# The first stage's operations, recorded and issued in the order of a planner inside the kernel

## The chip, the cores and the metric

One core of one Trainium2 chip runs the whole program. The metric is the device time of one execution in microseconds (us); lower is better. Three executions of the kernel before took 850.84, 848.12 and 849.52 us: the median is 849.52 us. One more execution was taken with the hardware profiler, and all rows below come from it.

The engines have the profile's names: PE is the matrix engine (PEld its weight loads), DVE the vector engine, ACT the activation engine, POOL the general one, SP the queue that issues most of the DMAs. Each takes its instructions strictly in the order of its own list; an instruction that waits holds up all that stand behind it.

## The reference, cut to what matters

Four layers stand one after the other on x of 2048 positions and 512 channels, each added to x:

```python
x = A_q
x = x + _A_ref(_layernorm(x), A_k, A_v, A_shift_k, A_ssm_k, A_ssm_D)
x = x + _B_ref(_layernorm(x), B_log_A_real, B_A_imag, ...)
x = x + _A_ref(_layernorm(x), A_k, A_v, A_shift_k, A_ssm_k, A_ssm_D)
x = x + _B_ref(_layernorm(x), B_log_A_real, B_A_imag, ...)
# _A_ref: kv = (4-tap causal convolution of k) * v
#         y  = long causal convolution of kv with ssm_k (FFT of 4096) + kv * ssm_D;  q * y
# _B_ref: K[d, l] = 2 Re sum_n C[d, n] exp(A[d, n] dt[d] l), l = 0 .. 2047, n = 0 .. 127
#         y  = long causal convolution of u with K + u * D_skip
```

The convolution inside A and the kernel K of B are the same in both rounds, since neither depends on x.

## The kernel before, in words

All lines are those of the kernel before. Long convolutions are done as Fourier transforms by matrix products. Channels come in four quarters of 128 (NQ), a quarter's frequencies in eight chunks (NCH). There are three parts:

- **The prologue** (lines 354 to 444) turns the parameters of B into four rows per mode, splits each into a high and a low half (`split`, line 378) and writes them to DRAM (`rows_d`, line 383).
- **The first stage** (lines 447 to 745) runs two streams of work, which `run_steps` (line 924) records in turns, two steps of one and three of the other.
- **The rest** (from line 748) is the first round's B, then the second round's A and B, and takes what the first stage wrote to DRAM (`spec`, `ya_d`, `x1_d`).

The first stage's streams:

- `stream()` (line 599) makes K. 64 **taps** in 16 groups of four: `load_rows` (line 470) loads a group's rows (`raw`) and casts them to `rw` on DVE (line 478); `mags` (line 480) makes magnitudes, a matmul and an Exp on ACT (line 488), six for every eight taps; `angles` (line 493) makes a tap's angles in a bank `pa` of PSUM by two matmuls (lines 497 and 502) with a rounding on DVE between them (line 501); `waves` (line 505) takes one Abs and five sines on ACT (lines 509 to 514); `products` (line 518) multiplies twice on POOL (lines 525 and 526) and once on DVE (line 527, which frees the bank `pa`, of which there are two); `contract` (line 531) sums over the modes on PE (line 539), and after a group's fourth tap writes the group to DRAM (`kdram`, line 551). After each 16 taps `spectrum_quarter(1, q)` (line 249) loads the quarter back (`kk`, line 221), adds D_skip on POOL (line 265), transforms it (lines 179, 188, 197), copies it out on ACT (line 278) and writes it as `spec` (line 279).
- `diagonal()` (line 708) does A: first `spectrum_quarter(0, q)` of ssm_k, beside 16 groups of the short convolution, `gated` (line 620: eight multiplications and additions in SBUF, four on POOL and four on DVE, all eight on POOL for the first group), and the statistics of x (`row_stats`, line 643); then `convolution(0, ...)` (line 284): spectra of kv (lines 179 and 188), the products with `kab` (loaded at line 294; lines 306, 308, 309), the way back (lines 211, 318, 332, 338) and the gate (lines 692, 693, 704). `ln_rows` (line 674) runs four times within it: it loads four rows of x for each partition (`xr`, one buffer), normalizes them by four instructions on ACT (line 679) and writes them to `ln_d` (line 681).

Exps and sines need different tables on ACT; `after` (line 113) keeps each set together by an edge in the order, without a wait.

**What sets the order.** Each call of an operation is traced at once, in the order in which the two streams are recorded. A scheduler of the framework (`schedule_with_timeline_sim=True`, line 982) then sets the place of each instruction on its engine by a priority and a model of times of its own, over the whole program, and puts in the semaphores. PSUM and SBUF tiles with the same tag share a few buffers: `f1` (two buffers, line 451) holds in turn the results of lines 179, 197, 211 and 486.

Of the kernel before, what the change touches and what calls it, by code (L numbers as in the profile page):

```python
# [100 lines left out]


@with_exitstack
def kernel(ctx: ExitStack, tc: tile.TileContext, out, x_in, kv_in, ssmk_in, ssmd_in,
                           la_in, ai_in, cr_in, ci_in, ldt_in, ldtb_in, dsk_in,
                           w1_in, w2_in, mm_in, w4_in, minus_in, tt_in, tg1_in, tg2_in, dbg=None):
    nc = tc.nc
    V, S, G, T = nc.vector, nc.scalar, nc.gpsimd, nc.tensor

    def sbuf(stack, name, side="left"):  # L110
        return stack.enter_context(tc.tile_pool(name=name, bufs=1, side=side, reuse_waits="tile"))

    def after(ins, first):
        tc.add_manual_dep(ins.ins, first.ins.name,
                          mybir.DependencyInfo(mybir.DependencyClass.NoSync, mybir.DependencyReason.DATA),
                          reason="activation tables")

# [11 lines left out]
    GL = 2  # L129
# [87 lines left out]
    def by_half(tile_, rows, store=False):  # L217
        src = rows.rearrange("(a b n) y -> b n a y", a=2, b=2)
        for b in range(2):
            ends = tile_[64 * b:64 * b + 64], src[b]  # L220
            nc.sync.dma_start(*(ends[::-1] if store else ends))

# [26 lines left out]
    def spectrum_quarter(which, q, src, pool, zlast, zb):  # L249
        z = pool.tile([128, 64, 32, 2], F32, name="zk", tag="z", bufs=zb)  # L250
        dr = pool.tile([1, 128], F32, name="dr", tag="dr", bufs=1)
        nc.sync.dma_start(dr, (ssmd_in, dsk_in)[which][:, 128 * q:128 * q + 128])
        for g in range(4):
            kk = pool.tile([128, 512], F32, name="kk", tag="kk", bufs=(NKK, 2)[which])
            by_half(kk, src[4 * q + g])
            d = dr[:, 32 * g:32 * g + 32]
            if which == 0:
                kv = kk.rearrange("p (t c) -> p t c", c=32)
                view = lambda ps_, j, n: kv[ps_, :, j:j + n]
            else:  # L260
                kv = kk.rearrange("p (i t c) -> p t i c", i=4, c=8)
                view = lambda ps_, j, n: kv[ps_, :, j // 8:(j + n) // 8, :]
                d = d.rearrange("p (i c) -> p i c", c=8)

            G.tensor_add(kv[0:1, 0], kv[0:1, 0], d)
            fwd_group(view, z, 32 * g, zlast[-zb] if len(zlast) >= zb else None)
            yield
        for c in range(NCH):
            if c % 2 == 0:
                pu, ins = f2_pair(z, c)  # L270
                if c == NCH - 2:
                    zlast.append(ins)

            if which == 1 and q == NQ - 1:
                pc = wk.tile([128, CK * 128], F32, name="pc", tag="m1", bufs=NM1 // 2)
            else:
                pc = pool.tile([128, CK * 128], F32, name="pc", tag="pc", bufs=2)
            S.copy(pc, pu[:, c % 2].rearrange("p k c -> p (k c)"))  # L278
            nc.sync.dma_start(spec[which][q][c], pc)
            yield  # L280
# [3 lines left out]
    def convolution(which, pools, steps, finish, lag, ahead, nk, ns, nw, inplace, zlast=None, late_step=None, first_b=False):  # L284
# [3 lines left out]
        def load(s):  # L288
            q, c = divmod(s, NCH)
            pool = pools["conv"]  # L290
            kab = pool.tile([128, 2, CK, 128], F32, name="kab", tag="kab", bufs=nk)
            eng = G if first_b and s < GL else nc.sync
            rows = spec[which][q][c].rearrange("(f v) x -> f (v x)", v=2)
# [69 lines left out]
    dt = gp.tile([128, 4], F32, name="dt")  # L363
    nc.sync.dma_start(dt, ldt_in)
    nc.sync.dma_start(flat(cr), cr_in)
    nc.sync.dma_start(flat(ci), ci_in)
    nc.sync.dma_start(flat(la), la_in)
    nc.sync.dma_start(flat(ai), ai_in)
    nc.sync.dma_start(w1, w1_in)
    dt2 = gp.tile([128, NQ, 32], F32, name="dt2")  # L370
# [7 lines left out]
    def split(i, v, eng):  # L378
# [3 lines left out]
        eng.tensor_sub(hl[:, 1], v, hl[:, 0])  # L382
        nc.sync.dma_start(rows_d[k].rearrange("q (h r x) g n -> r (q h) x (g n)", h=2, r=2)[r]
                          .rearrange("a (c p) y -> a c (p y)", p=2),
# [56 lines left out]
    nc.sync.dma_start(flat(dt2), ldtb_in[:, None, :].to_broadcast([4, 32, 128]))  # L441
    S.activation(dt2, dt2, AF.Exp)
# [8 lines left out]
    psum["f1"] = (pp, 2)  # L451

    wk = sbuf(gctx, "wk")
    kp = sbuf(gctx, "spec_k")
# [15 lines left out]
    def load_rows(gi):  # L470
        if gi in rows:
            return
        raw = wk.tile([128, 2, 128], F32, name="raw", tag="raw", bufs=2)
        q, g = divmod(gi, 4)
        for k in range(2):
            nc.sync.dma_start(raw[:, k, :], rows_d[k][q, :, g, :])
        rows[gi] = wk.tile([128, 2, 128], F32R, name="rw", tag="rw", bufs=2)
        V.tensor_copy(rows[gi], raw)
# [52 lines left out]
    def contract(gi, k):  # L531
# [18 lines left out]
        for i4 in range(4):  # L550
            nc.sync.dma_start(
                kdram[gi].rearrange("(s n) (i x) -> i n s x", n=32, i=4)[i4],
# [57 lines left out]
    with ExitStack() as actx:  # L610
# [9 lines left out]
        def gated(grp, onpool):  # L620
# [16 lines left out]
            e[7].tensor_mul(u, u, kt(19))  # L637
            nc.sync.dma_start(kv_d[grp], u.rearrange("p t c -> p (t c)"))
            yield
# [12 lines left out]
        def steps_a(q):  # L652
# [3 lines left out]
            def load(g):  # L656
                us[g] = ap.tile([128, 16, 32], F32, name="u", tag="kk", bufs=NKK)
                nc.sync.dma_start(us[g].rearrange("p t c -> p (t c)"), kv_d[4 * q + g])

# [14 lines left out]
        def ln_rows(j):  # L674
# [5 lines left out]
            for q in range(NQ):  # L680
                nc.sync.dma_start(ln_d[q][:, 4 * j:4 * j + 4, :], xr[:, :, 128 * q:128 * q + 128])

        xqs = {}

        def load_x(q):
            xqs[q] = ap.tile([128, 16, 128], F32, name="xq", tag="xq", bufs=1)
            nc.sync.dma_start(xqs[q], ln_d[q])

# [6 lines left out]
        def stats_a(q, c):  # L695
# [3 lines left out]
            if c == 6:  # L699
                nc.sync.dma_start(x1_d[q], xqs[q])  # L700

        def finish_a(q, g, po):
            ya = ap.tile([128, 512], F32, name="ya", tag="pc", bufs=2)
            S.copy(ya, po.rearrange("p t c -> p (t c)"))
            nc.sync.dma_start(ya_d[:, :, 4 * q + g].rearrange("k p x -> p k x"), ya.rearrange("p (k x) -> p k x", k=4))
            update_a(q, g, po)

        def diagonal():
            kvs = kv_steps()
            for q in range(NQ):  # L710
                for i, _ in enumerate(spectrum_quarter(0, q, ssmk_in, ap, zlast, ZA)):
# [4 lines left out]
                    if q == 0 and i < 4:  # L716
                        nc.sync.dma_start(w2[:, 8 * i:8 * i + 8], w2_in[:, 8 * i:8 * i + 8])
                    if q == 2 and i < 4:
                        ins = nc.sync.dma_start(mm[:, 8 * i:8 * i + 8], mm_in[:, 8 * i:8 * i + 8])
                        after(ins, zlast[0])  # L720
                    if q == 3 and i == 0:
                        after(nc.sync.dma_start(w4, w4_in), zlast[0])
                    next(kvs, 0)
# [19 lines left out]
        for _ in range(4):  # L743
            next(diag)
        run_steps([(stream(), RT), (diag, RD)])


# [3 lines left out]
    def gated_update(buffer, spare, rnd):  # L751
        yas = []
        for k in range(4):
            ya = buffer(k)
            nc.sync.dma_start(ya.rearrange("p g t c -> p (g t c)"), ya_d[k].rearrange("p g x -> p (g x)"))
            yas.append(ya)
# [47 lines left out]
    for q in range(NQ):  # L804
        nc.sync.dma_start(x[:, :, 128 * q:128 * q + 128], x1_d[q])
    last_root[0] = normalizer(0, 16, st_all)
# [180 lines left out]
```

## Time and profile before

| | |
|---|---|
| median of three runs | 849.52 us (848.12 to 850.84) |
| profiled execution, whole | 858.07 us |
| its span, from first to last instruction | 856.2 us |
| mean granted PE clock | 0.821 |
| DVE, ACT, POOL busy | 541.8, 433.9, 401.0 us |
| moved by DMA | 147.35 MB, mean 172 GB/s |

The first stage's last operations run at about 600 us. A row of a timeline or of the chain of waits begins with its start and its length in us. A group's row gives line, engine, operation, result<-operands and count, then busy time, mean length (ns), and the idle time just ahead of the group with what ended it. A row of stretches gives for each engine the busy time and, in brackets, the count, and then the granted clock of PE, the share of DMA and GB/s. A source row gives shortest, median and longest length in ns.

### The profile page before, as it was taken

Reading aid. Unit: us, or ns where it says so; the run is one execution under the profiler, and the core shown is the slowest. Engines: PE = TensorE matmul, PEld = TensorE weight load, DVE = VectorE, ACT = ScalarE, POOL = GpSimd, SP = SyncE. Lnnn points to the kernel's source line nnn. Section 1 sums busy time; section 2 is a strip of 40 time slices with the busy share of each in tenths; the row PEclk is TensorE's granted clock in tenths of the full one; section 3 lists DMA queues with packets and bytes.
Section 4 is the critical chain, followed back from the end, with each engine's and each line's share of the span. In section 5 each row is a group of like instructions: output and inputs, shape, how many; then the busy total and the mean of one; then the engine's idle time right before and its main releaser. Section 6 shows DMA issues by size and latency. Waiting matters only on the chain.

```text
span 856.2 us, 20760 instructions
## 1 busy us (share of the span) xinstructions
PE 564.1 (66%) x8440; PEld 325.6 (38%) x8440; DVE 541.8 (63%) x931; ACT 433.9 (51%) x800; POOL 401.0 (47%) x362
## 2 busy tenths in 40 slices
PE   2336664556747765358978667886379895469985
PEld 0014233323424422136534434552136562136562
DVE  7858888783544443134777562477457798987874
ACT  3126344435636783385774527552566341856431
POOL 4859989943332622227734422542035351045451
PEclk9999999657776556757997977797689998689998
DMA  9865844543345335765656553554978573127874
GB/s 249 200 179 156 280 138 155 172 146 121 108 142 179 104 85 137 177 192 158 215 148 226 185 163 121 162 173 122 279 241 283 200 248 99 49 57 257 259 233 88
DMA packets 77635, 147.35 MB, mean 172 GB/s; under 512 B 8668, under 2 KB 37732, under 8 KB 74980
## 3 DMA queue, kind: packets, MB, share of 16 engines
q1 hardware_dynamic: 76676, 143.60, 54.9%
q0 software_dynamic: 864, 2.43, 0.8%
q8 instruction: 67, 1.10, 0.5%
q14 instruction: 28, 0.23, 0.1%
HBM read 101.95 MB, written 44.04 MB: 171 GB/s over the span
## 4 chain that ended last, share of the span: by engine, by line
PE 23%; DVE 14%; ACT 14%; issue 10%; DMA 9%; POOL 2%; SPq 1%; POOLq 0%; ACTq 0%; DVEq 0%
PE pi L211 7%; PE pu L197 4%; DMA kab<-spec 4%; PE po L338 3%; PE pf L179 3%; PE pk L539 2%; DVE w L332 2%; PE pa L502 2%; DVE vv L309 2%; ACT m L488 2%; DVE zu L188 2%; DMA kk<-kdram 2%; ACT ab L509 1%; DMA ln_d<-xr 1%; DVE x L774 1%
## 5 line engine op out<-in xcount | busy, mean ns | idle before, releaser
L308 POOL TENSOR_TENSOR sw<-sw,kab 128x512 f32<-128x512 f32 x96 | 121.0, 1281 | 141.7 <-ACT sw L306 131.8
L525 POOL TENSOR_TENSOR xy<-tt,m 128x512 f32<-128x512 f32 x64 | 76.2, 1191 | 139.6 <-issue 69.7
L527 DVE TENSOR_TENSOR e<-pa,m 128x512 f32<-128x512 f32 x64 | 43.8, 684 | 109.4 <-ACT pa L514 109.3
L211 PE MATMUL pi<-vv,mm 64*64 64x128 f32 x1536 | 89.1, 288 | 9.5 <-DVE vv L309 3.0
L211 PE MATMUL pi<-sw,mm 64*64 64x128 f32 x1536 | 88.5, 285 | 5.3 <-POOL sw L308 3.1
L309 DVE TENSOR_TENSOR vv<-pu,kab 128x512 f32<-128x512 f32 x96 | 62.1, 680 | 44.7 <-ACT sw L306 28.9
L539 PE MATMUL pk<-xy,e 128*32 128x64 f32 x2048 | 61.4, 271 | 39.7 <-POOL xy L526 26.8
L509 ACT ACTIVATE ab<-pa 128x512 f32<-128x512 f32 x64 | 38.2, 597 | 97.3 <-PE pa L502 96.8
L179 PE MATMUL pf<-kk,w 64*128 64x512 f32 x128 | 62.6, 960 | 30.9 <-DMA kk<-ssmk_in 20.4
L497 PE MATMUL pa<-tt,rw 64*128 64x512 f32 x64 | 42.0, 659 | 61.2 <-DVE e L527 61.1
L526 POOL TENSOR_TENSOR xy<-tt,m 128x512 f32<-128x512 f32 x64 | 79.1, 1237 | 0.0
L179 PE MATMUL pf<-u,w 64*128 64x512 f32 (+1 forms) x200 | 64.3, 713 | 19.7 <-ACT pc L278 9.7
L188 DVE STREAM_TRANSPOSE zu<-pf 128x512 f32<-128x512 f32 x96 | 62.3, 689 | 22.9 <-PE pf L179 22.7
L539 PEld LDWEIGHTS pk<-xy,e 128*32 128x32 f32 x2048 | 45.3, 139 | 78.8 <-POOL xy L526 41.5
L488 ACT ACTIVATE m<-pm 128x1024 f32<-128x1024 f32 x48 | 47.1, 1027 | 50.7 <-PE pm L486 50.5
L338 PE MATMUL po<-w,w 128*64 128x512 f32 x192 | 60.0, 714 | 18.1 <-DVE xq L693 10.8
L197 PE MATMUL pu<-zu,w 64*64 64x128 f32 x1536 | 61.4, 293 | 15.3 <-DVE zu L188 13.7
L211 PEld LDWEIGHTS pi<-vv,mm 64*64 64x64 f32 x1536 | 57.3, 140 | 34.6 <-issue 20.8
L306 ACT COPY sw<-pu 128x1024 f32<-128x1024 f32 x48 | 48.7, 1015 | 37.7 <-PE pu L197 37.5
L197 PEld LDWEIGHTS pu<-zu,w 64*64 64x64 f32 x1536 | 50.3, 145 | 38.5 <-issue 21.0
L211 PEld LDWEIGHTS pi<-sw,mm 64*64 64x64 f32 x1536 | 61.2, 142 | 8.4 <-issue 4.6
L318 ACT COPY ie<-pi 128x1024 f32<-128x1024 f32 x32 | 32.4, 1013 | 60.6 <-PE pi L211 60.6
(141 smaller groups left out, 1125.9 us busy)
## 6 DMA issues: line engine op xcount, KB each, us to landing
kab<-spec SPq DMA_DIRECT2D x94, 512.0 KB
spec<-pc SPq DMA_DIRECT2D x64, 256.0 KB
kvt<-kv_in SPq DMA_DIRECT2D x32, 312.0 KB
kk<-ssmk_in SPq DMA_DIRECT2D x32, 128.0 KB
xr<-x_in SPq DMA_DIRECT2D x8, 512.0 KB
kv_d<-u SPq DMA_DIRECT2D x16, 256.0 KB
kdram<-ks SPq DMA_DIRECT2D x64, 64.0 KB
kk<-kdram SPq DMA_DIRECT2D x32, 128.0 KB
```

Of the source, the lines that this page charges most:

```text
L179: yield T.matmul(o, w1[half, :], rhs, start=True, stop=True)
L188: V.transpose(zr[:, :, r], pf[..., r].rearrange("p a x t -> p x a t"))
L197: ins = T.matmul(pu[64 * o:64 * o + 64, odd, i, :], w2[64 * h:64 * h + 64, k, :], z[64 * h:64 * h + 64, :, k, :], start=True, stop=True, t ...
L211: ins = T.matmul(pi[64 * o:64 * o + 64, odd, i, :], mm[64 * h:64 * h + 64, (c + odd) * CK + i, 64 * part:64 * part + 64], w[64 * h:64 * h ...
L306: swapped[0] = S.copy(vvs[s // 2][1], pus[0])
L308: G.tensor_mul(wb[:, c % 2], wb[:, c % 2], kabs[s][:, 1])
L309: V.tensor_mul(wa[:, c % 2], pus[0][:, c % 2], kabs[s][:, 0])
L338: ins = T.matmul(po[64 * a:64 * a + 64], w4, ws[g][:, :, 16 * a:16 * a + 16, :].rearrange("p x t r -> p t x r"), start=True, stop=True, ti ...
L488: i = S.activation(m, pm, AF.Exp)
L525: G.tensor_mul(xy[:, :, :, 32:64], tt[:, 0:2, :, 1:33], m1[:, :, 32:64][:, None].to_broadcast([128, 2, 8, 32]))
L526: G.tensor_mul(xy[:, :, :, 0:32], tt[:, 0:3:2, :, 0:32], m1[:, :, 0:32][:, None].to_broadcast([128, 2, 8, 32]))
L539: T.matmul(pk[32 * i4:32 * i4 + 32, 2 * k + i, :], e2[:, r, 4 * i + i4, :], xy[:, r, 4 * i + i4, :], start=r == 0, stop=r == 1, tile_posit ...
```

## The change

Five names stand for the engines now (V, S, G, T, and Q for the SP queue) and hand every call to a `Planner`. Up to line 452 a call is still traced at once, and recorded as well. From there to the end of the first stage (`planner.deferred = True`) it is recorded alone, with the regions of the tiles that it reads and writes. At the end of the stage `planner.flush()` plans, and traces the recorded calls in the plan's order; an edge from each operation to the one before it on its engine fixes this order for the framework's scheduler. Matmuls that follow each other in the record and write the same tile are one operation. The arithmetic, the tiles, their buffers and the DMAs are the same. Later parts go as before.

The plan is a list schedule: the operation that can start first is taken, and of two on one engine that can start at the same time the one recorded first. A tile of a tag gets its buffer in the order of the record. A DMA of the SP queue also waits for one of eight lanes; DVE and POOL exclude each other for operations that have only SBUF operands.

```diff
+class Planner:
+    RELEASE = {"V": 34, "S": 60, "G": 90, "T": 80, "D": 27}
...
+    def edge(self, ins, first):
+        self.tc.add_manual_dep(ins, first.name,
+                               mybir.DependencyInfo(mybir.DependencyClass.NoSync, mybir.DependencyReason.DATA),
+                               reason="order of the plan")
...
+    def record(self, key, name, a, k):
...
+        if (key == "T" and last is not None and last.engine == "T" and last.ins is None
+                and last.calls[-1][1][0].tensor.name == outs[0].tensor.name):
+            op = last
+        else:
+            op = Op(key, len(self.ops))
+            self.ops.append(op)
+        op.calls.append((name, a, k))
+        for x, w in [(x, True) for x in outs] + [(x, False) for x in ins]:
+            if not self.tc.is_my_tile(x.tensor):
+                continue
+            (p0, p1), m = self.region(x)
+            past = self.tiles.setdefault(x.tensor.name, [])
+            for o, q0, q1, mm_, ww in past:
+                if (w or ww) and o is not op and q0 < p1 and p0 < q1:
+                    e = min(len(m), len(mm_))
+                    if (m[:e] & mm_[:e]).any():
+                        op.before.add(o)
...
+        if not self.deferred:
+            op.ins = getattr(self.engines[key], name)(*a, **k).ins
+        return op
...
+    def cost(self, op):
...
+        if name == "dma_start":
+            size = 4 * n * max(1, aps[0].ap[0][1]) if aps[0].space != DRAM else 4 * int(np.prod([c for _, c in aps[0].ap]))
+            return (450 if op.engine == "D" else 600), 1500 + size / 290, size
...
+        if op.engine == "T":
+            total, each = 0, 0
+            for _, b, _ in op.calls:
+                d = free(b[2]) * (1 if b[2].dtype == F32R else 4) / 2.4
+                area = b[1].ap[0][1] * free(b[1]) / 16384
+                total, each = total + d * area, max(each, d)
+            return max(total, each), max(total, each) + 230, 0
+        if op.engine == "V":
+            alone = len(big) == 1 and not psum[0] and name in ("tensor_copy", "tensor_scalar", "tensor_scalar_mul")
+            o = 60 + n * (0.52 if alone else 1.06)
+            return o, o + 85, len(big) > 1 and not any(psum)
+        if op.engine == "S":
+            o = n / 1.2 + (50 if all(psum) else 184)
...
+            return o, o + 105, 0
+        o = 100 + 2.2 * n if name.startswith("tensor_tensor") or name in ("tensor_mul", "tensor_add", "tensor_sub") else 100 + 0.9 * n
+        return o, o + 50, n > 1
...
+    def plan(self):
...
+                    if e == "D":
+                        t = max(t, min(lanes))
+                    if costs[n][2] and e in "VG":
+                        t = max(t, lock["G" if e == "V" else "V"])
+                    if pick is None or (t, n) < pick:
+                        pick = (t, n)
+                if pick is not None and (best is None or pick[0] < best[0]):
+                    best = (pick[0], pick[1], e)
...
+            if e == "D" or op.calls[0][0] == "dma_start":
+                server = max(server, t + o) + extra / 290
+                end[n] = max(t + o + 1500, server + 1200)
...
+        return sorted(range(len(ops)), key=lambda n: (start[n], n))
+
+    def flush(self):
+        last = {}
+        for n in self.plan():
+            op = self.ops[n]
+            if op.ins is not None:
+                continue
+            for i, (name, a, k) in enumerate(op.calls):
+                ins = getattr(self.engines[op.engine], name)(*a, **k).ins
+                if i == 0:
+                    if op.engine in last:
+                        self.edge(ins, last[op.engine])
...
+            op.ins = last[op.engine] = ins
+        self.deferred, self.ops, self.tiles = False, [], {}
...
-    V, S, G, T = nc.vector, nc.scalar, nc.gpsimd, nc.tensor
+    planner = Planner(tc, nc)
+    V, S, G, T, Q = [planner.engine(e) for e in "VSGTD"]
...
+    planner.deferred = True
     wk = sbuf(gctx, "wk")
...
         run_steps([(stream(), RT), (diag, RD)])
+        planner.flush()
```

More of the change, by code (lines that the diff above doesn't have):

```diff
@@ L220, in by_half @@
             ends = tile_[64 * b:64 * b + 64], src[b]
-            nc.sync.dma_start(*(ends[::-1] if store else ends))
+            Q.dma_start(*(ends[::-1] if store else ends))
     off = cpool.tile([128, 16], F32, name="off")
@@ L278, in spectrum_quarter @@
             S.copy(pc, pu[:, c % 2].rearrange("p k c -> p (k c)"))
-            nc.sync.dma_start(spec[which][q][c], pc)
+            Q.dma_start(spec[which][q][c], pc)
             yield
@@ L475, in load_rows @@
         for k in range(2):
-            nc.sync.dma_start(raw[:, k, :], rows_d[k][q, :, g, :])
+            Q.dma_start(raw[:, k, :], rows_d[k][q, :, g, :])
         rows[gi] = wk.tile([128, 2, 128], F32R, name="rw", tag="rw", bufs=2)
@@ L699, in stats_a @@
             if c == 6:
[L700 removed]
+                Q.dma_start(x1_d[q], xqs[q])
         def finish_a(q, g, po):
```

187 lines of the change are left out of this document (162 added, 25 removed).

## The prediction

> **What bounds the kernel now.** I began with the page's busy times, to see whether an engine is full.
>
> ```profile
> PE 564.1 (66%) x8440; PEld 325.6 (38%) x8440; DVE 541.8 (63%) x931; ACT 433.9 (51%) x800; POOL 401.0 (47%) x362
> ```
>
> None is. So I cut the span into stretches: prologue, the taps 1 to 15 beside the short convolution, then groups of about eight taps, the long convolution of A among them, and two stretches behind the first stage.
>
> ```profile
> 0.00:45.00 45.00, 11.95 (x16) 3.18 (x16) 34.11 (x41) 11.47 (x17) 29.55 (x39) 1.00 0.88 226
> 45.00:188.00 143.00, 78.00 (x794) 42.55 (x794) 114.37 (x119) 58.47 (x121) 121.91 (x93) 0.90 0.59 174
> 188.00:247.00 59.00, 41.20 (x538) 22.32 (x537) 25.59 (x47) 35.16 (x74) 22.18 (x25) 0.71 0.40 128
> 247.00:308.00 61.00, 42.08 (x531) 25.24 (x533) 25.67 (x50) 41.17 (x77) 19.14 (x19) 0.60 0.39 122
> 308.00:372.00 64.00, 27.26 (x319) 13.73 (x319) 19.96 (x38) 33.18 (x70) 17.32 (x18) 0.63 0.61 157
> 372.00:584.00 212.00, 169.81 (x2755) 102.13 (x2751) 125.53 (x222) 124.69 (x226) 98.67 (x88) 0.82 0.53 170
> 584.00:600.00 16.00, 9.81 (x104) 3.34 (x92) 11.09 (x17) 2.83 (x5) 1.52 (x3) 0.68 0.46 140
> 600.00:645.00 45.00, 23.74 (x352) 13.03 (x352) 23.11 (x70) 25.88 (x54) 9.93 (x8) 0.73 0.82 260
> 645.00:722.00 77.00, 66.89 (x1376) 43.26 (x1376) 61.82 (x120) 33.73 (x45) 33.00 (x27) 0.96 0.61 206
> ```
>
> The columns are PE, PEld, DVE, ACT, POOL, then clock, DMA share, GB/s. POOL is nearly full from 45 to 188 (121.9 of 143). After that no engine is: from 188 to 372 the fullest, PE, works 110.5 of 184 us, and that at a clock of 0.6 to 0.7. Here the order of waiting, not an engine, sets the pace. The stretch from 308 to 372 is the emptiest. ACT's timeline shows why:
>
> ```profile
> 328.57 2.92 ACT L679 ACTIVATE xr<-xr,nb,rs 128x512 f32<-128x512 f32 x4 [9.78 <-DMA raw<-rows_d]
> ...
> 346.11 2.93 ACT L679 ACTIVATE xr<-xr,nb,rs 128x512 f32<-128x512 f32 x4 [8.11 <-DMA xr<-x_in]
> ...
> 364.66 2.93 ACT L679 ACTIVATE xr<-xr,nb,rs 128x512 f32<-128x512 f32 x4 [10.08 <-DMA kk<-kdram]
> ```
>
> Three times the normalization of x (line 679) stands on ACT ahead of its data, 28.0 us together, with the sines of the next taps behind it.
>
> **The change part by part.** It removes and adds no operation; it moves the first stage's. I compared the order of the changed program's instructions with the old, engine by engine. Behind the first stage each engine's list is the same. The order in which the results of lines 179, 197, 211 and 486 pass through their two PSUM buffers is the same too, so the large interleaving of the streams stays. What moves is each engine's order in detail, and that of the SP queue.
>
> *Start.* These rows carry it (the first is POOL's first operation of the stage, the last the first cast of a tap's rows):
>
> ```profile
> 13.02 0.51 POOL L265 TENSOR_TENSOR kk<-kk,dr 1x32 f32<-1x32 f32 x1 [1.35 <-DMA kk<-ssmk_in]
> ...
> 15.15 0.68 DVE L411 TENSOR_TENSOR ai<-ai,y 128x512 f32<-128x512 f32 x1
> ...
> 32.17 0.67 DVE L433 SCALAR_TENSOR_TENSOR ph<-ph,ci 128x512 f32<-128x512 f32 x1
> ...
> 37.45 2.28 SPq L383 DMA_DIRECT2D rows_d<-hl  x2
> ...
> 47.04 1.54 SPq L476 DMA_DIRECT2D raw<-rows_d  x2
> ...
> 52.71 1.30 DVE L478 CAST rw<-raw 128x256 fp32r<-128x256 f32 x1
> ```
>
> Between L411 and L433 DVE did stage work, and its own operations were stretched. The grouped rows from 17 to 40 us show two operations of one kind at two lengths:
>
> ```profile
> L636 DVE TENSOR_TENSOR u<-u,kvt 128x512 f32<-128x512 f32 x1 | 1.8, 1754 | 0.0
> ...
> L635 DVE TENSOR_TENSOR kvt<-kvt 128x512 f32<-128x512 f32 x1 | 0.6, 643 | 0.0
> ```
>
> I read 1.75 us as 0.64 plus a wait for POOL. In the changed order DVE finishes all its prologue before any stage work. From L411's end, 15.8, eight operations of at most 0.68 us come to at most 5.4: L433 ends at about 21 instead of 32.8, and the last rows go out at about 24 instead of 39.7. On SP the raw rows then stand behind a store that waits for the first group of the short convolution (three POOL operations in turn with four of DVE from 24 on: about 30) and five loads, so they go out at about 33.5; with the 5.7 from 47.04 to 52.71 their cast comes at 39 instead of 52.7.
>
> A wait is added here. The six memsets (lines 459, 460) now stand on POOL ahead of the short convolution, and one waits for L433, since the tile lies in memory that the prologue frees. The planner knows nothing of this wait. Behind it queue lines 265 and 629 to 637, and for 265 wait PE (179) and DVE (188). POOL so begins its stage work at about 21 instead of 13.
>
> *Taps 1 to 26.* If DVE waits for POOL in operations on SBUF, the two are one resource. POOL's own lengths:
>
> ```profile
> L525 POOL TENSOR_TENSOR xy<-tt,m x64: 1156/1176/1631, 68.3 to 580.0; 128x512 f32<-128x512 f32 x64
> ...
> L637 POOL TENSOR_TENSOR u<-u,kvt x16: 1251/1650/1800, 35.6 to 183.2; 128x512 f32<-128x512 f32 x16
> ```
>
> and the taps in each stretch (POOL's count of line 525):
>
> ```profile
> 60.00:125.00 65.00, 9.38 (x8) 1.00 0.63 186
> 125.00:188.00 63.00, 9.08 (x7) 0.78 0.53 161
> 188.00:247.00 59.00, 10.56 (x9) 0.71 0.40 128
> ```
>
> All 16 groups of the short convolution need 68 POOL operations at 1.25 (85 us) and 60 DVE operations at 0.64 (38). Before, they were done at 188, with 15 taps at 2 x 1.18 (35): 158 us of this resource in the 175 from 13 to 188, 90% full. Then it stood mostly idle, and tap 24 came at 247, tap 26 at about 263 (187 us for 24, 7.8 a tap). In the changed order the last of these operations stands behind tap 26. Demand: 85 + 38 + 26 x 2.36 = 184, from 21 on. Full it ends at 205, at 90% at 225, at 75% at 266. I take 87%, 233, against 263: **-30 us**, with +3 and -58 as ends; the start's earlier cast is in it.
>
> [...]
>
> *Normalization of x.* In the changed ACT order 25 to 40 instructions stand between one group of line 679 and the next, four or five taps with their sines and copies; the wait shown took 8 to 10 us. One buffer serves all four groups, but a round (328.57 to 346.11) is 17.5 us, and a tap takes 7.8, so four cover it. Of the 28.0 us I take 22, because what ACT did late some others also had to wait for: **-22 us**, ends -28 and -10.
>
> *Copies of the spectra.* Line 278 waits for its own stores:
>
> ```profile
> L278 ACT COPY pc<-pu 128x512 f32<-128x512 f32 x64 | 34.8, 586 | 26.7 <-DMA spec<-pc 17.6 <-PE pu L197 9.0
> ```
>
> Two buffers, and before four copies stood next to each other in many places. Now singles and pairs stand between a tap's sines, with few runs of three or four. I take half of 17.6: **-9 us**, ends 0 and -17.6.
>
> *Everything else.* Better packing of taps 27 to 64 has its bound in ACT: it works 191 us of the 337 between 263 and 600 (three quarters of 41.2, then 33.2, 124.7 and 2.8). At 75% that is 255, 82 less, so at most 51 beyond the two terms above. Against it stands what the planner prices too low, on the chain of waits:
>
> ```profile
> 358.57 6.11 DMA kk<-kdram
> ...
> 483.46 7.34 DMA kab<-spec
> ```
>
> Its formula gives a transfer the larger of 1.5 us after the issue and 1.2 us after a server of 290 bytes a ns: about 2.4 for kk's two halves and 3.0 for kab. The instructions that take them are 2 to 4 us late by the plan. I take 0 for the two together, ends -51 and +40.
>
> Sum: -30 - 22 - 9 + 0 = **-61 us**. Against the profiled execution's 858.07 (its span of 856.2 and 1.9 around it) that is 797; the median of the runs is 8.6 lower, so I forecast **789 us**, with 765 to 815 as its own range.
>
> **The rivals.** *PE speeds up.* The clock was 0.60 to 0.63 where PE worked 42 of 61 and 27 of 64 us, 0.96 where it worked 66.9 of 77. A stage without ACT's three stops keeps PE busier, the clock rises, and matmuls shorten; then ACT at 75% bounds taps 27 to 64, 255 instead of 337 us: -82, with -30 at the start -112: 738. Against it: from 45 to 188 PE was granted 0.90 and 1.00 at 12 of 45, so emptiness alone does not lower it. [...]
>
> *The stage's chain stays.* The two buffers keep their order, and a tap's loop through the two banks `pa` is untouched. If taps go on at 7.8 us each and only the fixed stops go, the gain is 10 for line 679 and 12 in the first part (184 us at 80% full end at 251): 827.
>
> *The planner's DMA prices decide (slower).* The place: instructions that now stand in a fixed spot behind loads, lines 265 and 308 on POOL, 309 on DVE, 179 on PE. Some 80 tile loads (16 kk of taps, 32 kab, 16 raw, 16 u) are 3 us late by the plan. Each that falls on the chain costs 3 us, since each engine's list is fixed. With 20 on the chain the gain of 61 is gone; with 30 it is 90 - 61 = 29 slower: 878. For it speaks
>
> ```profile
> L265 POOL TENSOR_TENSOR kk<-kk,dr 1x32 f32<-1x32 f32 x32 | 10.1, 317 | 89.9 <-DMA kk<-kdram 56.1 <-DMA kk<-ssmk_in 12.7 <-issue 9.7
> ```
>
> where POOL stood 56 us in the old order. Against it: POOL has slack after tap 26, and the loads are issued as soon as a buffer is free in either order.
>
> *It does not do what it says.* The edges hold every operation of the stage in the changed lists; this one I give nothing.
>
> **How the numbers follow.** Forecast, 765 to 815: 0.52. PE speeds up, 720 to 765: 0.20. Chain stays, 815 to 847: 0.10. Within 0.3% (2.5 us, about what a measurement of this kernel can tell from no change): 0.03. Slower, mostly 852 to 878: 0.15. So faster 0.82, same 0.03, slower 0.15. The range 735 to 852 leaves out a quarter of the second case (0.05) and nearly all of the slower one (0.15).
>
> **What would show it.** The first cast of line 478 at about 39 instead of 52.7; tap 26 (line 525) at about 233 instead of 263; the short convolution spread over 26 taps; line 679 with no wait above 3 us; less than 10 us of line 278 behind its stores; the stage's last gate (line 693) at about 540 instead of 600; the rest as long as before, 256 us. It would be wrong if POOL stands longer than 56 us for kk, if the memsets hold POOL far beyond 21 us, or if PE's clock between 200 and 400 goes above 0.9; then the gain is larger.

## The result, and the profile after

Four executions of the changed kernel took 799.61, 793.69, 799.24 and 801.45 us: the median is **799.42 us**, against 849.64 us for the kernel before in the same runs. The ratio is 0.9399, with a 95% interval of 0.9348 to 0.945. The profiled execution took 799.61 us with a span of 797.6. The forecast was 789, its own range 765 to 815.

The busy times on the page of the changed kernel:

```profile
PE 551.8 (69%) x8440; PEld 321.3 (40%) x8440; DVE 516.9 (65%) x931; ACT 432.9 (54%) x800; POOL 391.1 (49%) x362
```

The same operations run, 58.6 us of span have gone, and no engine is full now either. What the engines do is nearly the same; what went is waiting. The stretches of the changed kernel (PE, PEld, DVE, ACT, POOL, then clock, DMA share, GB/s):

```profile
0.00:45.00 45.00, 13.24 (x16) 3.50 (x16) 26.26 (x42) 11.35 (x17) 26.05 (x37) 1.00 0.80 224
45.00:188.00 143.00, 91.92 (x1050) 51.25 (x1052) 93.65 (x126) 83.12 (x173) 105.66 (x91) 0.63 0.60 170
188.00:247.00 59.00, 41.74 (x529) 23.68 (x527) 40.10 (x64) 27.99 (x56) 39.34 (x34) 0.68 0.56 165
247.00:308.00 61.00, 44.49 (x576) 23.79 (x576) 34.42 (x63) 45.60 (x98) 28.41 (x29) 0.66 0.55 163
308.00:372.00 64.00, 48.19 (x787) 30.66 (x791) 28.91 (x46) 46.34 (x85) 31.50 (x29) 0.71 0.71 212
```

From 45 to 188 us ACT now does 83.1 us of work instead of 58.5, and DVE is busy 93.7 instead of 114.4. The empty stretch from 308 to 372 is fuller: PE 48.2 instead of 27.3, ACT 46.3 instead of 33.2. The clock lies between 0.63 and 0.71 from 45 to 372 us.

In the changed trace all recorded operations have one line, L319, so I go by tiles. Three groups of the changed kernel that answer to waits of before:

```profile
L319 POOL TENSOR_TENSOR kk<-kk,dr 1x32 f32<-1x32 f32 x32 | 9.5, 301 | 19.3 <-DMA kk<-kdram 19.3
...
L319 ACT COPY pc<-pu 128x512 f32<-128x512 f32 x64 | 35.4, 587 | 13.3 <-PE pu L319 13.3
...
L319 ACT ACTIVATE xr<-xr,nb,rs 128x512 f32<-128x512 f32 x16 | 11.7, 801 | 1.6 <-DMA xr<-x_in 1.0 <-DVE nb L319 0.6
```

The normalization of x waits 1.6 us instead of 28.0. The copies of the spectra no longer wait for their stores at all (17.6 before). POOL stands 19.3 us for the reloaded kk instead of 56.1.

**Where along the stage the time went.** A tap's last operation on POOL is the second `xy`, so POOL's count of `xy` is a clock of the stage: 2 are one tap, 32 are 16. For the old order I take a second profiled execution (experiment e1, whose lists are those of before), since the first one, 858.07 us, lies above every other execution of that order. The old order, then the changed one:

```profile
0.00:70.50 70.50, 2.75 (x2) 0.99 0.78 209
70.50:195.50 125.00, 38.52 (x30) 0.55 0.58 177
195.50:271.50 76.00, 23.09 (x20) 0.68 0.39 128
271.50:574.00 302.50, 88.36 (x76) 0.78 0.53 164
```

```profile
0.00:58.40 58.40, 2.31 (x2) 1.00 0.76 208
58.40:165.50 107.10, 36.95 (x30) 0.58 0.57 163
165.50:240.80 75.30, 24.13 (x20) 0.68 0.61 177
240.80:519.00 278.20, 88.22 (x76) 0.74 0.60 185
```

The stage's last gate in the old order (e1), then in the changed one:

```profile
589.84 0.69 DVE L177 TENSOR_TENSOR xq<-xq,po 128x512 f32<-128x512 f32 x1
```

```profile
546.02 0.69 DVE L319 TENSOR_TENSOR xq<-xq,po 128x512 f32<-128x512 f32 x1
```

| stretch | old (e1) | changed | difference |
|---|---|---|---|
| start to the end of tap 1 | 70.5 | 58.4 | -12.1 |
| taps 2 to 16 | 125.0 | 107.1 | -17.9 |
| taps 17 to 26 | 76.0 | 75.3 | -0.7 |
| taps 27 to 64 | 302.5 | 278.2 | -24.3 |
| last tap to the end of the last gate | 16.5 | 27.7 | +11.2 |
| all that follows | 250.5 | 250.9 | +0.4 |

The sum is -43.4, from a span of 841.0 to 797.6. The last cuts, 574.0 and 519.0, lie 1.0 us behind the end of tap 64 in both kernels, which moves no difference. The medians say -50.2; two single executions differ from them by some us each way. Nearly all of the gain lies in the first 16 taps and in taps 27 to 64, and 11 us of it is given back when the stage closes.

### The profile page after: what moved, and what is told of

The parts are those of the page before. It is cut to its first block, busy times and chain, and to the rows that moved or that the text cites. A ratio compares the mean times of both kernels' runs of the same rounds, so it can differ in the third digit from the quotient of the medians.

```text
span 797.6 us, 20671 instructions
## 1 busy us (share of the span) xinstructions
PE 551.8 (69%) x8440; PEld 321.3 (40%) x8440; DVE 516.9 (65%) x931; ACT 432.9 (54%) x800; POOL 391.1 (49%) x362
## 3 DMA queue, kind: packets, MB, share of 16 engines
q1 hardware_dynamic: 76676, 143.60, 58.4%
## 4 chain that ended last, share of the span: by engine, by line
PE 36%; DVE 23%; ACT 17%; issue 9%; DMA 9%; POOL 4%; SPq 1%; DVEq 0%; ACTq 0%; POOLq 0%
PE pf L319 6%; PE pa L319 5%; PE pu L319 5%; PE pk L319 4%; ACT m L319 4%; PE pi L319 4%; PE pi L177 3%; DMA kab<-spec 3%; ACT tt L319 2%; PE pu L177 2%; PE po L319 2%; PE pf L177 2%; DVE zu L177 2%; DVE x L177 2%; DVE w L177 2%
## 5 line engine op out<-in xcount | busy, mean ns | idle before, releaser
L319 POOL TENSOR_TENSOR xy<-tt,m 128x512 f32<-128x512 f32 x128 | 151.6, 1205 | 98.5 <-ACT tt L319 55.2
L319 PE MATMUL pf<-kk,w 64*128 64x512 f32 x128 | 62.7, 955 | 36.6 <-DMA kk<-ssmk_in 19.5
L319 ACT ACTIVATE m<-pm 128x1024 f32<-128x1024 f32 x48 | 47.1, 1023 | 67.6 <-PE pm L319 50.8
L319 PE MATMUL pk<-xy,e 128*32 128x64 f32 x2048 | 57.5, 274 | 17.4 <-POOL xy L319 13.6
L319 DVE STREAM_TRANSPOSE zk<-pf 128x512 f32<-128x512 f32 x64 | 42.1, 693 | 40.3 <-PE pf L319 40.2
L319 DVE TENSOR_TENSOR e<-pa,m 128x512 f32<-128x512 f32 x64 | 43.6, 683 | 35.4 <-ACT pa L319 25.3
L319 ACT ACTIVATE ab<-pa 128x512 f32<-128x512 f32 x64 | 38.2, 597 | 51.2 <-PE pa L319 50.5
L319 POOL TENSOR_TENSOR sw<-sw,kab 128x512 f32<-128x512 f32 x32 | 40.6, 1279 | 51.7 <-ACT sw L319 29.8
L319 PE MATMUL pa<-tt,rw 64*128 64x512 f32 x64 | 42.8, 672 | 32.3 <-DVE e L319 29.7
L177 DVE TENSOR_TENSOR vv<-pu,kab 128x512 f32<-128x512 f32 x64 | 41.2, 679 | 33.8 <-ACT sw L177 30.5
L319 PEld LDWEIGHTS pk<-xy,e 128*32 128x32 f32 x2048 | 44.3, 143 | 43.7 <-POOL xy L319 28.1
L319 PE MATMUL pa<-y,minus 128*128 128x512 f32 x64 | 42.6, 671 | 26.2 <-DVE y L319 26.2
L319 DVE TENSOR_SCALAR y<-pa 128x512 fp32r<-128x512 f32 x64 | 43.6, 683 | 25.6 <-PE pa L319 25.5
L319 PE MATMUL pu<-zk,w 64*64 64x128 f32 x1024 | 50.7, 360 | 11.0 <-ACT pc L319 5.2
L319 POOL TENSOR_TENSOR u<-u,tb 128x512 f32<-128x512 f32 x32 | 44.4, 1390 | 23.4 <-DVE tb L319 12.7
L177 PE MATMUL pf<-u,w 64*128 64x512 f32 (+1 forms) x136 | 39.3, 665 | 23.3 <-ACT u L177 15.1
L177 PE MATMUL pi<-vv,mm 64*64 64x128 f32 x1024 | 53.6, 275 | 1.2 <-DVE vv L177 1.1
L177 PE MATMUL pi<-sw,mm 64*64 64x128 f32 x1024 | 52.8, 270 | 0.7 <-issue 0.7
L319 PEld LDWEIGHTS pu<-zk,w 64*64 64x64 f32 x1024 | 42.6, 185 | 26.0 <-issue 12.8
L319 ACT ACTIVATE tt<-pa 128x256 f32<-128x256 f32 x128 | 44.7, 387 | 10.9 <-PE pa L319 7.1
```

Of the source, the lines that this page charges most:

```text
L177: op.ins = getattr(self.engines[key], name)(*a, **k).ins
L319: ins = getattr(self.engines[op.engine], name)(*a, **k).ins
```

## The experiments

All ratios are against the kernel before, run on the same chip beside the experiment.

### e1: calls recorded, nothing planned

```diff
-    planner.deferred = True
```

> Calls are recorded, but each is traced at once; no plan. Every engine's list is then that of before. If the gain comes from the plan's order alone: 849 us, within 4. If the recording itself moves the time: elsewhere. The profile is a second one of the old order: it tells whether the 8.6 us by which the first profiled execution lay above the median belong to a place (then the last gate comes near 592 instead of 600) or to the whole span.

One execution: 842.89 us; the kernel before 846.16 (840.45 to 849.83). So nothing speaks for the recording as the cause, as far as one execution can tell. The last gate ends at 590.5 instead of 599.9, and what follows takes 250.5 us instead of 256.3: the first profile's surplus lay partly in the stage (taps 27 to 64 took 7.8 us longer) and partly behind it.

### e2: the plan's order without its edges

```diff
                 if i == 0:
-                    if op.engine in last:
-                        self.edge(ins, last[op.engine])
+                    pass
```

> The calls are traced in the plan's order, but no edge fixes it; the framework's scheduler places them again. Theory A (the places of single instructions count, and the edges hold them): the groups of the x normalization stand close together on ACT again and wait again, and the short convolution is drawn ahead again; 830 to 850 us. Theory B (the order of the trace is enough): 795 to 805.

879.46 us, ratio 1.0417 (1.0358 to 1.0476): slower than the kernel before, and outside both forecasts. Calls in the plan's order, placed again by the framework's scheduler, bring the waits back in another form. Two groups of this kernel on ACT and the first of its waits:

```profile
L319 ACT COPY pc<-pu 128x512 f32<-128x512 f32 x64 | 34.8, 587 | 34.8 <-DMA spec<-pc 19.5 <-PE pu L319 12.1 <-PE pk L319 1.7
L319 ACT ACTIVATE xr<-xr,nb,rs 128x512 f32<-128x512 f32 x16 | 11.7, 802 | 16.5 <-DMA kdram<-ks 9.1 <-DMA xr<-x_in 7.5
```

```profile
DVE e L319 <- ACT pa L319: 136.9, 32, 16.0
```

So the fixed lists carry the gain; the order of tracing alone does not.

### e3, e8, e4: the prices of the plan

The plan's own figures are worked out while the kernel is built, so they can be read off without a chip. Its DMA server is busy 502 of the 510 us of the plan. The reason is the size: the larger free size of either side times the partitions of the result. A load such as `kab` has a source with one more dimension ahead, and counts twice. The plan so gives `kab` 12.7 us in the median from issue to landing, `kk<-kdram` 7.6, `spec<-pc` 7.2. The chip, in the changed kernel (KB each, median us to landing):

```profile
kab<-spec SPq DMA_DIRECT2D x94, 512.0 KB, 5.4
spec<-pc SPq DMA_DIRECT2D x64, 256.0 KB, 2.2
...
kk<-kdram SPq DMA_DIRECT2D x32, 128.0 KB, 2.9
```

e3 has the first of these edits, the result's size (the server is then busy 344 us); e8 has the first two, with a longer landing; e4 has all three, with PE's prices nearer to the trace:

```diff
-            size = 4 * n * max(1, aps[0].ap[0][1]) if aps[0].space != DRAM else 4 * int(np.prod([c for _, c in aps[0].ap]))
+            size = 4 * int(np.prod([c for _, c in aps[0].ap]))
...
-                end[n] = max(t + o + 1500, server + 1200)
+                end[n] = max(t + o + 3000, server + 2700)
...
-                d = free(b[2]) * (1 if b[2].dtype == F32R else 4) / 2.4
+                d = free(b[2]) * (2 if b[2].dtype == F32R else 4) / 1.6
```

> A DMA's size in the plan is that of its result; before, the larger number of elements for each partition of either side was multiplied by the partitions, so most loads counted twice. In the plan as changed the DMA server is busy 502 of 510 us, with the sizes mended the plan ends at 435. Theory C (the plan was held by a DMA limit that the chip doesn't have: kab is priced at 12.7 us by the plan and lands in 5.4): the stage ends 25 to 55 us earlier, 745 to 775 us. Theory D, the prediction's rival (DMAs are priced too low, and what takes their data is late): with still lower prices more instructions stand ahead of their data, 805 to 830. Theory E (the taps' chain through the two banks pa sets the pace, whatever the plan): 795 to 805.

> The kernel e3 (mended sizes) with 3.0 instead of 1.5 us from a DMA's issue to its landing, PE's prices as in the changed kernel. It tells which of the two prices made e4 16 us faster than e3. The prediction's rival (DMA prices too low, loads late): 755 to 762, all of it from the landing. If PE's price does it (0.21 us in the plan for an angle matmul that takes 0.67): 768 to 776.

> As the kernel with mended sizes, and two more prices nearer to the trace: matmuls at 1.6 instead of 2.4 columns a ns with the 32-bit rounded type at half rate (0.64 us for 512 columns; measured 0.67), and 3.0 instead of 1.5 us from a DMA's issue to its landing. The plan ends at 469. Theory C, with the remaining slip a matter of prices: 735 to 770 and not slower than the mended sizes alone. Theory E: 795 to 805. If prices of PE and landing matter little: within 5 us of the mended sizes alone.

| | us | ratio (95%) | plan's end |
|---|---|---|---|
| changed kernel | 799.42 | 0.9399 (0.9348 to 0.945) | 510 |
| e3, sizes | 773.29 | 0.9155 (0.9111 to 0.92) | 435 |
| e8, sizes and landing | 762.68 | 0.9003 (0.8964 to 0.9043) | 439 |
| e4, sizes, landing and PE | 757.27 | 0.8952 (0.8896 to 0.9007) | 469 |

Theory C holds: the plan was held by a DMA limit that the chip did not show (`kab` 12.7 us by the plan, 5.4 on the chip), and mending the sizes alone wins 26 us by the medians. These are of different groups of runs, in which the kernel before differs by some us; by the two ratios it is 21 us. Of the stage itself, 23.6 us went (last gate at 523.1 instead of 546.7). The landing wins 10.6 more by the medians, 13 by the ratios; e4's further 5.4 lies within overlapping intervals. An earlier end by the plan is no forecast: e4's plan ends 34 us later than e3's, and e4 is faster. That it is faster because its prices are nearer to the trace is the likely reading; e7 below shows that nearer is not always faster.

### e5: the kernel before, with the normalization of x spread

```diff
-        LN0, LNS = -8, 3
+        LN0, LNS = -12, 6
...
-                S.activation(xr[:, i], xr[:, i], AF.Identity, ...)
+                after(S.activation(xr[:, i], xr[:, i], AF.Identity, ...), last_sin[0])
```

> The kernel before with one thing changed: each group of the x normalization on ACT comes behind the sines of a later tap, so that some 45 instructions of ACT stand from one group to the next instead of about 20. Prediction's step (its 28.0 us of idle time on ACT in three places, of which 22 are won): 820 to 836 us, with waits of under 10 us left at line 679. If what ACT does next would have waited for something else anyway: 840 to 850, the waits gone or moved, the time not.

826.08 against 848.02 us, ratio 0.9765 (0.9712 to 0.9818): **-21.9 us** (15 to 24 by the interval of the ratio), for one move in the old order. The groups stand apart on ACT and wait for nothing:

```profile
L679 ACT ACTIVATE xr<-xr,nb,rs 128x512 f32<-128x512 f32 x16 | 11.8, 801 | 0.0
```

### e6, e7, e11, e10: POOL and DVE in the short convolution

e6 is e4 with the short convolution wholly on DVE; e7 is e4 with no exclusion in the plan; e11 is both; e10 is the changed kernel, doubled sizes and all, with no exclusion. The first two edits put the convolution on DVE, the third takes the exclusion out:

```diff
-        KVE = 0b10010110
+        KVE = 0
...
-                            for _ in gated(grp, 255):
+                            for _ in gated(grp, 0):
...
-                    if costs[n][2] and e in "VG":
+                    if False:
```

> The kernel e4 with all eight operations of each group of the short convolution on DVE (0.64 us each) instead of four on POOL (1.25 us each). If POOL and DVE exclude each other in SBUF, a POOL operation costs their shared time twice what a DVE one does: 68 x 0.6 = 41 us less demand before tap 26; the plan, which has this rule, ends at 442 instead of 469; the chip 735 to 752 against 757, tap 24 at 185 to 205 instead of 215. If they work beside each other, DVE alone gets 43 us more in a stretch where it is two thirds full: 757 to 775, tap 24 later than 215.

> The kernel e4 with the exclusion of DVE and POOL left out of the plan (its own end then 440 instead of 469). If the chip does exclude them, the order is laid for a machine that isn't there: 757 to 775, and DVE's additions and multiplications in SBUF show lengths near 1.8 us more often. If it doesn't: 730 to 750.

> e6 and e7 together: mended sizes, nearer prices of PE and landing, no exclusion in the plan, the short convolution wholly on DVE. The plan ends at 434 (e6: 442, e7: 440). If the two remedy the same loss (POOL's demand ahead of tap 26): 728 to 738, as each alone. If they add: 715 to 725. If without POOL's share the taps' chain is the bound already in e6: 735 to 742.

> The changed kernel with only the exclusion left out of the plan, DMA sizes counted twice as before. In e7 this was worth 22 us, all of it ahead of tap 24, where DVE's operations of the short convolution then take their place in line. If the plan's rule starves them here too: tap 24 at 190 to 200 instead of 216, 775 to 785 us. If the doubled DMA sizes hold the start anyway: 793 to 803.

| | us | ratio (95%) | end of tap 24 | end of the last gate |
|---|---|---|---|---|
| changed kernel | 799.42 | 0.9399 (0.9348 to 0.945) | 216 | 546.7 |
| e10 | 795.08 | 0.9384 (0.9325 to 0.9444) | 194 | 535.1 |
| e4 | 757.27 | 0.8952 (0.8896 to 0.9007) | 215 | 495.5 |
| e6 | 737.58 | 0.8705 (0.8645 to 0.8765) | 185 | 471.4 |
| e7 | 735.06 | 0.869 (0.8637 to 0.8742) | 192 | 471.6 |
| e11 | 733.82 | 0.8647 (0.8588 to 0.8706) | 189 | 471.1 |

e6 came as expected for engines that exclude each other (tap 24 at 185 us). e7 did not: with the rule taken out of the plan the chip is as fast. The lengths of one operation of the short convolution on DVE (shortest, median, longest in ns) in the kernel before, in the changed one, in e7, and in e9 (the kernel before with all of the short convolution on DVE, see below):

```profile
L635 DVE TENSOR_TENSOR kvt<-kvt x15: 643/1634/1758, 31.6 to 178.0; 128x512 f32<-128x512 f32 x15
```

```profile
L319 DVE TENSOR_TENSOR kvt<-kvt x15: 691/1164/3952, 29.0 to 231.2; 128x512 f32<-128x512 f32 x15
```

```profile
L319 DVE TENSOR_TENSOR kvt<-kvt x15: 679/955/1658, 29.8 to 201.5; 128x512 f32<-128x512 f32 x15
```

```profile
L635 DVE TENSOR_TENSOR kvt<-kvt x16: 677/684/1653, 31.3 to 163.3; 128x512 f32<-128x512 f32 x16
```

DVE's operation does wait for POOL's: in the old order its median was 1.63 us, its shortest 0.64, and with POOL's part of the short convolution taken away (e9) the median is 0.68. The rows show it one by one: in the first profile of the kernel before 38 of DVE's 60 operations of the short convolution took over 0.85 us, each of these ended 0.55 us behind the end of an operation of POOL's, and none of the other 22 lay within one. In the changed kernel it is 23 of 60, at the same 0.55 us. POOL's wait as well: 35 of its 68 took over 1.35 us in that first profile, and each of these ended 1.12 to 1.14 us behind the end of one of DVE's, of the other 33 only four. Over all 60 of DVE's the median is 0.70 us in e4 and 0.98 in e7, so the order without the rule does collide more often, as expected, and is faster even so. The likely reason lies in the list. The plan lets whatever can start first go first, so an operation that must wait for the other engine's is put off as long as another can start; the short convolution ends at 241 us in e4 and at 205 in e7. A collision mostly costs about 1 us (1.63 against 0.64), in single cases over 3 (3.95 in the changed kernel's row); avoiding it in the list cost more. That reading of the list is argued; the 22 us are measured.

The two remedies do not add (e11). The likely reason is that DVE is then nearly full ahead of tap 26. Two stretches of e11, DVE third:

```profile
45.00:100.00 55.00, 36.70 (x434) 20.31 (x432) 53.81 (x74) 31.76 (x67) 24.85 (x21) 0.70 0.78 221
100.00:160.00 60.00, 46.65 (x577) 25.49 (x577) 55.52 (x81) 43.06 (x88) 30.05 (x28) 0.62 0.69 195
```

e10 reaches tap 24 some 22 us earlier, and in the end cannot be told from the changed kernel. Of the 22 us, 11.6 are left at the last gate, and the rest of the program, 250.9 us in the changed kernel, takes 259.9; why it does is not shown. In e6, e7 and e11 the rest is longer too (259.3 to 262.7 us), and there a part is work of the first stage that was still to be done: behind e11's last gate PE has 128 matmuls of the stage's last spectrum left (7.7 us), against 48 (1.7 us) in the changed kernel. In e10 only 32 are left, so this does not explain it. Nor does an early last gate alone: in e3, with the gate at 523.1, the rest takes 248.6 us. PE's work behind the gate in e11, 188.8 us:

```profile
471.00:733.00 262.00, 188.79 (x3483) 117.35 (x3480) 186.12 (x405) 126.85 (x213) 90.79 (x80) 0.86 0.58 191
```

and in the changed kernel, 179.4 us:

```profile
547.00:797.00 250.00, 179.38 (x3400) 110.43 (x3389) 184.67 (x402) 126.44 (x212) 90.39 (x79) 0.90 0.59 193
```

e11 has the lowest median, 65.6 us under the changed kernel; e6 and e7 cannot be told from it.

### e9 and e12: the kernel before, one part of the first 26 taps at a time

e9 moves the short convolution wholly to DVE in the kernel before (as in e6). e12 holds each of its groups behind a tap (`last_e` lists the operations of line 527 recorded so far):

```diff
...
-            e[0].tensor_mul(u, kt(3), sk(0))
+            first = e[0].tensor_mul(u, kt(3), sk(0))
+            if last_e and e[0] is V:
+                after(first, last_e[-1])
```

> The kernel before with all eight operations of each group of the short convolution on DVE. The prediction counted POOL and DVE as one resource, 90% full from 13 to 188 us, with 158 us of demand; this takes 68 x 0.61 = 41 us of it away. If that resource set the pace there: tap 16 at 160 to 175 us instead of 196, and 815 to 835 us in all. If POOL and DVE work beside each other, or the taps' own chain sets the pace: tap 16 at 190 or later, 843 to 860.

> The kernel before with one thing changed: the first operation on DVE of each group of the short convolution is held, by an edge in DVE's order, behind the line-527 operation of the last tap recorded before it. Its 15 groups then stand one to every second tap or so, up to tap 27, as in the changed kernel, instead of ahead of tap 15. If it was this crowding on DVE and POOL that held the first taps (prediction's step of 30 us, whatever the resource behind it): tap 16 at 165 to 182 us instead of 195, tap 26 at 240 to 258 instead of 271, and 818 to 838 us in all. If the step came from the earlier start (first cast at 45 instead of 53) and the detailed order alone: tap 16 at 188 or later, 842 to 855.

e9: 846.62 us, ratio 0.9971 (0.9927 to 1.0015), no change; tap 16 ends at 199 us. POOL's load from 45 to 188 fell from 122.2 us to 41.2, DVE's rose a little, and the taps kept their pace. The old order (e1), then e9:

```profile
45.00:188.00 143.00, 77.10 (x795) 42.85 (x795) 113.82 (x120) 59.19 (x123) 122.15 (x100) 0.63 0.58 175
```

```profile
45.00:188.00 143.00, 72.80 (x791) 41.28 (x791) 117.75 (x165) 58.54 (x121) 41.24 (x35) 0.66 0.61 178
```

This does not mean that the two engines' load was harmless. From 60 to 160 us, while the short convolution runs, e9 has DVE almost without a pause; the load went from POOL to DVE and did not leave the stretch. The old order (e1), then e9, DVE third and POOL fifth:

```profile
60.00:160.00 100.00, 59.04 (x668) 34.34 (x668) 82.29 (x81) 48.82 (x103) 92.47 (x71) 0.60 0.61 181
```

```profile
60.00:160.00 100.00, 52.34 (x555) 29.57 (x553) 95.54 (x130) 45.11 (x87) 31.34 (x26) 0.60 0.63 184
```

A full DVE alone does not hold the taps either: in e6 it is busy 92.7 us of the same 100, and tap 16 ends at 132 us. There the short convolution lasts until 223 us, in e9 until 167, so what DVE does first matters.

e12: 859.92 us, ratio 1.0154 (1.0078 to 1.023), slower by 1 to 2%. Its clock of `xy`:

```profile
0.00:66.60 66.60, 2.31 (x2) 1.00 0.78 207
66.60:182.70 116.10, 37.28 (x30) 0.65 0.52 155
182.70:287.40 104.70, 24.38 (x20) 0.58 0.46 140
```

The first 16 taps end 13 us earlier than in e1 (taps 2 to 16 take 116.1 us instead of 125.0), the next ten take 104.7 us instead of 76.0. Crowding did hold the first taps, and spreading alone costs more in the next ones than it wins; why they are so slow stays open.

## Why the prediction was right, and where it was not

**Normalization of x, -22.** Right in mechanism and size: the wait is gone, and the one move alone is worth 21.9 us (e5).

**Taps 1 to 26, -30.** The size came out: -30.7 between the two profiles above. My two dates for tap 26 were both early by some 8 to 10 us: 263 for the old order, which I had extrapolated from 7.8 us a tap instead of counting (it is 271.5 to 273), and 233 for the new one (240.8). The reason I gave is shown only in part. That the single operations wait for each other is shown (the 0.55 and 1.12 us between their ends, and e9's 0.68 against 1.63 us), and that crowding held the first taps too (e12). My sum, in which POOL and the short convolution on DVE are one resource and nothing else counts, does not stand: by it e9's 41 us less demand had to bring tap 16 to 160 to 175 us, and it came at 199. The sum had left out all else that DVE does, and e9 has DVE busy 95.5 of 100 us, so e9 does not tell whether the two engines' waits or DVE's own load set the pace. Nor is spreading alone the answer (e12). What the trace shows is an earlier start, -12.1 to the end of tap 1, and -17.9 in taps 2 to 16. That those 17.9 us need all engines' lists to be laid out together is the likeliest reading of e9, e12 and e2, but only argued; which of the moves carries them stays open.

**The start.** These rows of the changed kernel answer to my dates, on DVE, on POOL and on SP:

```profile
21.39 0.68 DVE L177 SCALAR_TENSOR_TENSOR ph<-ph,ci 128x512 f32<-128x512 f32 x1
...
45.07 0.48 DVE L319 CAST rw<-raw 128x256 fp32r<-128x256 f32 x2
```

```profile
22.13 0.25 POOL L319 MEMSET tt<- 128x8 f32 x4 [1.58 <-DVE ph L177]
```

```profile
36.45 2.01 SPq L319 DMA_DIRECT2D raw<-rows_d  x4
```

L433 ended at 22.1 (forecast 21), and the memsets waited for it and let POOL go at 22.4, as said. The rows went out at 36.5 (33.5), and the cast came 8.6 us behind them, at 45.1, where I had taken the 5.7 of the old order: 39 was 6 us too early. It cost little, since tap 1 was still 12 us earlier.

**Copies of the spectra, -9.** The wait is gone, 17.6 to 0. Its worth was not measured apart. Taps 27 to 64 gained 24.3 us where the two terms together said 31; with 21.9 shown for the one, little is left for the other.

**Everything else, 0.** Here stood two errors. Behind the last tap 11.2 us were lost, which no term had. And I said that the plan prices DMAs too low. For a single transfer that is so (`kab` with its true size: about 3.0 us by the formula, 5.4 on the chip), and 1.5 us more landing won 10.6 us (e8). But I had left out the server's queue in the same formula: with the doubled sizes it is full, and transfers came out 2.4 to 3.3 times too dear (12.7 against 5.4 us, 7.6 against 2.9, 7.2 against 2.2). The sign of the rival was wrong: with the sizes mended, that is with lower prices, the kernel is 21 to 26 us faster (e3).

**From the sum to the forecast.** The step that missed is the last: "the median of the runs is 8.6 lower, so I forecast 789". On the profile's own scale the sum gave 797, and the changed kernel's profiled execution took 799.61. But the 8.6 us were a peculiarity of the one execution of before; the changed kernel's profile lay at its median. Part of the gain that I counted in that execution, in taps 27 to 64, was not in the typical one: in e1 line 679 waits 26.1 us instead of 28.0, and line 278 13.2 us for its stores instead of 17.6. On the first profile's own scale the agreement, 61 against 58.6, is partly luck: the 11.2 us lost at the close and 5.4 won behind it (256.3 to 250.9) were in no term.

**Rivals.** PE did not speed up: the clock between 188 and 372 us was 0.66 to 0.71, the angle matmuls of line 502 took 0.67 us in the mean (0.68 before), and taps 17 to 26 took the same time. But the argument that I had set against this rival was not sound (see the last section). The chain through the two banks did not hold the stage at 827. The kernel does what it says, and only through its edges (e2).

## What to carry to other kernels

A list order that is worked out ahead is worth as much as its prices and its rules: compare the plan's own lengths, and how full its modelled resources are, with the trace, before judging the plan. Before a wait is counted as gain, undo or do that one move alone in the old kernel, as e5 does; before a "full resource" is believed, take load off it, and look where the load goes (e9). And where the profiled execution is slower than the runs, take a second profile before its surplus is carried over as a constant.

## What the runs showed of the hardware

The clock's row misled me more than it helped. From 45 to 188 us the old order shows a granted clock of 0.90 in the first profile and 0.63 in the second (e1), with PE busy 78.0 and 77.1 us and taps 2 to 16 at about 125 us in both. The lengths of the angle matmuls of line 502 (shortest, median, longest) tell which to believe. The first profile from 45 to 188 us and from 188 to 600, then e1 in the same two stretches:

```profile
L502 PE MATMUL pa<-y,minus x16: 792/796/796, 57.8 to 187.4; 128*128 128x512 f32 x16
...
L502 PE MATMUL pa<-y,minus x49: 494/505/796, 187.4 to 576.2; 128*128 128x512 f32 x49
```

```profile
L177 PE MATMUL pa<-y,minus x16: 502/796/797, 57.1 to 186.4; 128*128 128x512 f32 x16
...
L177 PE MATMUL pa<-y,minus x48: 494/513/797, 190.8 to 566.8; 128*128 128x512 f32 x48
```

Up to 188 us they take 0.80 us in the median in both executions, behind it about 0.51. So PE was as slow there in the first execution as in the second. In the first profile the records of the clock begin at 150.5 us, and every stretch ahead of them reads 1.00; the 0.90 from 45 to 188 and the 1.00 from 60 to 125 are therefore no evidence, and the first profile's mean of 0.821 is too high for the same reason (in e1 the stretch up to 70.5 us still reads 0.99, the next 125 us read 0.55, and its mean is 0.785). The prediction's "emptiness alone does not lower it" rested on these rows. What lowers the clock is not shown here.

The angle matmuls of 512 columns in the rounded 32-bit type took 0.67 us, three times what the plan gives them (0.21). The changed kernel's two groups:

```profile
L319 PE MATMUL pa<-tt,rw 64*128 64x512 f32 x64 | 42.8, 672 | 32.3 <-DVE e L319 29.7
...
L319 PE MATMUL pa<-y,minus 128*128 128x512 f32 x64 | 42.6, 671 | 26.2 <-DVE y L319 26.2
```
